# A one-column exponential ahead of ScalarE's third q transfer in an attention and feed-forward kernel

## The chip, the cores and the metric

The kernel runs on one core of a Trainium2 chip. The metric is the device time of one execution in microseconds; lower is better. The time before is the median of three runs, 856.87 us (856.82 to 857.83).

## The reference

Eight batches of eight heads, 576 positions, 64 columns per head. The softmax of q runs over a head's columns, that of k over the positions; attention is linear, and its output goes through a feed-forward layer with a squared ReLU.

```python
q_s = exp(q - max(q, axis=-1)); q_s = q_s / (sum(q_s, axis=-1) + 1e-9)
k_s = exp(k - max(k, axis=2));  k_s = k_s / (sum(k_s, axis=2) + 1e-9)
kv = einsum('bhsd,bhse->bhde', k_s, v)
x = einsum('bhsd,bhde->bhse', q_s, kv)      # as 4608 tokens x 512
h = maximum(x @ w_in, 0.0)                  # w_in 512 x 2048
return (h * h) @ w_out                      # w_out 2048 x 512
```

q, k and v are float32. The weights arrive as float64 and are turned into float32 on the chip.

## The kernel before

Heads are worked on in pairs p = 0 to 3 of each batch b. A batch has 512 positions in main tiles (q_b_p, k_b_p, v_b_p: 128 partitions x 512) and 64 left over in tail tiles for all heads (qt_b, kt_b, v_tail). Every number of the feed-forward matmuls is carried as a rounded part and a rest (names ending in h and l: xh, xl, gh, gl), three matmuls for one product. A token tile has 512 tokens; for each block f of 128 columns of w_in, twelve matmuls make h, ScalarE and VectorE square it, and twelve make its share of acc. The last token tiles are computed from sums and differences of weight blocks (lines 1264 and 1776).

Weights come in 16 units u. Each is two halves of 512 KB (raw_u), which ScalarE scales, VectorE shifts and joins, GpSimd adds (w<-w,raw), ScalarE rounds and GpSimd splits (w<-w,w). Units 0 to 11 lie in the pool const, 12 to 15 in the pool late, which takes the place of the pool boot once the first batch's tiles are done with. SBUF pools are opened in the order const, att, cvt, ffn, tiny, boot (later late); tiny holds small statistics.

The first batch starts the kernel. For it, k's maximum over positions is taken from transposed keys:
- TensorE transposes k_0_p into PSUM (kT) and the tail kt_0 into ktT.
- `first_tail_max`: VectorE reduces ktT to ktm, and ScalarE copies ktT back over kt (two lines below); both read the same PSUM bank, and VectorE's reduction comes behind the copy.
- `first_max`: VectorE reduces kT to kc and joins ktm into it (kc<-kc,ktm).
- `first_exp`: ScalarE computes exp(kT + kc), with its sums.
- `q_max`, `q_exp`: VectorE takes the maximum over q (mx), GpSimd subtracts it (q<-q,mx), ScalarE takes the exponential.

```python
V.tensor_reduce(out=ktm, in_=ps[:, 0:2 * P].rearrange("p (n t) -> p n t", t=TL), op=ALU.max, axis=AX.X, n=256)
S.copy(out=kt, in_=ps[:, 0:2 * P], n=256)
```

The engines are V (VectorE, DVE), S (ScalarE, ACT), G (GpSimd, POOL), T (TensorE, PE) and Y (SyncE, SP). Nearly all transfers are issued by SP; the first batch's q and qt by ScalarE's queue, in the order q_0_0, qt_0 (two halves), q_0_1, q_0_2, q_0_3. Eight transfer semaphores (DMAHW0 to DMAHW7) go round over all issues, so an issue waits until the transfer that had its semaphore before has landed.

The instructions are not issued as they are written. Every call on an engine is recorded (line 100 is the recorder, which is why most rows of the profile bear that line), and a planner orders them by reckoned times: an instruction counts as a fixed part plus a part per column, for ScalarE

```python
V, S, G = Engine(plan, nc.vector, 0.14, 0.00108), Engine(plan, nc.scalar, 0.18, 0.00087), Engine(plan, nc.gpsimd, 0.1, 0.0021)
```

`plan.together()` records several calls as one step, and a list of seeds shifts the ranks of steps by their place in the record. Transfers on one queue keep the order in which they were recorded. Where TensorE would have nothing to do early on, a fixed number of dummy transposes (`idle<-ident`, line 1454) is put in, from the planner's times.

The function table of ScalarE is loaded by an instruction of its own, ACT_TABLE_LOAD, which the compiler puts ahead of the first instruction on ScalarE that is not a transfer.

Of the kernel before, what the change touches and what calls it, by code (L numbers as in the profile page):

```python
# [10 lines left out]
F32 = mybir.dt.float32  # L11
# [4 lines left out]
AF = mybir.ActivationFunctionType  # L16
# [320 lines left out]
def attention_ffn(  # L337
# [29 lines left out]
    P = 128  # L367
# [3 lines left out]
    NP = H // 2  # L371
# [40 lines left out]
    def pool(name, bufs, to=ctx, **more):  # L412
        return Pool(to.enter_context(tc.tile_pool(name=name, bufs=bufs, **more)), bufs)

    const, att, cvt = pool("const", 1), pool("att", 1), pool("cvt", 2)
    ffn, tiny = pool("ffn", 2), pool("tiny", 1)
# [13 lines left out]
    plan = Planner()  # L430

    V, S, G = Engine(plan, nc.vector, 0.14, 0.00108), Engine(plan, nc.scalar, 0.18, 0.00087), Engine(plan, nc.gpsimd, 0.1, 0.0021)
# [7 lines left out]
    ones = const.pool.tile([P, P], F32, tag="ones", name="ones")  # L440
# [100 lines left out]
    def pair_tile(b, p, shape, tag, dtype=F32):  # L541

        two = tag in ("ek", "v")
        pool = boot if b == 0 and p < NP - 1 - two else att
        return pool.tile(shape, dtype, tag=tag, name=f"{tag}_{b}_{p}", bufs=2 if two else None)
# [7 lines left out]
    def load_kq(b, p, which, queue=Y):  # L553
        turned = which == "k" and b == 0
        t = pair_tile(b, p, [P, C, 2, D] if turned else [P, 2, C, D], which)
        src = (k if which == "k" else q)[b, 2 * p:2 * p + 2, 0:M, :]
        to = "p c h d" if turned else "p h c d"
        queue.dma_start(out=t, in_=src.rearrange(f"h (p c) d -> {to}", c=C), kb=256)
        made[which, b, p] = t
# [20 lines left out]
    def load_v(b, p):  # L580
        t = pair_tile(b, p, [P, VW], "v")
        if b == 0:
            t = t[:, 0:2 * C * D].rearrange("p (h c d) -> p h c d", h=2, c=C)
            Y.dma_start(
                out=t, in_=v[b, 2 * p:2 * p + 2, 0:M, :].rearrange("h (p c) d -> p h c d", c=C),
                kb=256,
            )
            made["v", b, p] = t
            return
        t = t[:, 0:C * W].rearrange("p (c w) -> p c w", c=C)  # L590
        (G if b < TB else V).memset(t[:, :, D:D + 1].only("ones"), 1.0, n=4)
        for j in range(2):
            Y.dma_start(
                out=t[:, :, j * (D + 1):j * (D + 1) + D].only(j),
                in_=v[b, 2 * p + j, 0:M, :].rearrange("(p c) d -> p c d", c=C),
                kb=128,
            )
        made["v", b, p] = t
# [697 lines left out]
    load_tail_kq(0, "k")  # L1296
    load_tail_kq(0, "q", S)
    load_kq(0, 1, "k")
    for p in range(1, NP):
        load_kq(0, p, "q", S)  # L1300
    load_v(0, 0)
    load_tail_v(0)
    load_words(0)
# [703 lines left out]
```

## Time and profile before

| what | value |
|---|---|
| median of three runs | 856.87 us |
| the profiled execution: time | 858.72 us |
| the profiled execution: span | 856.92 us |
| mean granted clock of TensorE | 0.998 |
| TensorE busy | 843.8 us, 98% of the span |
| VectorE, ScalarE, GpSimd busy | 631.1, 424.2, 126.4 us |
| moved by DMA | 111.78 MB, mean 130 GB/s |

The profile is one execution. A row of its timeline gives the start and the length in microseconds from the span's start, the engine, the line, the operation, out<-in and how many were merged (x3); brackets hold how long the engine sat idle ahead of it and what ended that. An engine's name with q (ACTq, SPq) is its queue issuing a transfer. Buffer numbers are left out, so k stands for all tiles of k. The chain is followed back from the last instruction to what released it, step by step. A DMA row gives the size of a transfer and the microseconds from issue to landing.

### The profile page before, as it was taken

To read this page: it belongs to the slowest core of one execution; us is meant where nothing else is said; L and a number is where in the kernel's file an instruction comes from. 1 tells how busy PE (TensorE), PEld (TensorE's weight loads), DVE (VectorE), ACT (ScalarE), POOL (GpSimd) and SP (SyncE) were. 2 spreads that over 40 slices of the span, in tenths; PEclk is the share of its full clock that TensorE was granted. 3 is DMA by queue.
4 is the path that set the end of the run, shared out by engine and by line. 5 is a ranking of instruction groups with operands and counts; after the bars stand their busy time and mean duration, and the time that the engine had idled before them with its cause. 6 is when DMAs were issued, how large, how long until landed. Compare 5 with 4: busy or idle time off the path is not lost.

```text
span 856.9 us, 12691 instructions
## 1 busy us (share of the span) xinstructions
PE 843.8 (98%) x4356; PEld 697.1 (81%) x4356; DVE 631.1 (74%) x1241; ACT 424.2 (50%) x794; POOL 126.4 (15%) x154
## 2 busy tenths in 40 slices
PE   7899999999999999999999999999999999999997
PEld 6688888888888888888888888888888888888886
DVE  5898887776776677777686777776767756777985
ACT  4888864343534344433534344334533536666442
POOL 5789981000000000000000000000000000000000
PEclk9999999999999999999999999999999999999999
DMA  9991122323531443233432341132351039979565
GB/s 288 384 352 41 36 60 85 88 78 77 143 98 31 138 106 107 73 86 89 132 90 69 108 144 40 40 90 58 89 134 40 5 114 323 301 275 376 150 182 96
DMA packets 192752, 111.78 MB, mean 130 GB/s; under 512 B 130736, under 2 KB 175792, under 8 KB 192688
## 3 DMA queue, kind: packets, MB, share of 16 engines
q1 hardware_dynamic: 186768, 109.27, 43.2%
q10 hardware_dynamic: 5920, 1.71, 0.8%
q8 instruction: 34, 0.56, 0.3%
q14 instruction: 30, 0.25, 0.1%
HBM read 73.79 MB, written 36.57 MB: 129 GB/s over the span
## 4 chain that ended last, share of the span: by engine, by line
PE 92%; DVE 2%; POOL 1%; DMA 1%; ACT 1%; issue 0%; SPq 0%; DVEq 0%; ACTq 0%; POOLq 0%
PE h L100 35%; PE acc L100 35%; PE h L1264 9%; PE out L1776 8%; PE x L100 3%; PE kv L100 2%; DMA out_dram<-o 0%; DVE bst L100 0%; POOL w L100 0%; SPq L100 0%; POOL qn L100 0%; PE qT L100 0%; DMA bst<-bst 0%; DVE kvl L100 0%; DVE q L100 0%
## 5 line engine op out<-in xcount | busy, mean ns | idle before, releaser
L100 PE MATMUL h<-xh,w 128*128 128x512 f32 x896 | 296.6, 393 | 0.0
L100 PE MATMUL acc<-w,gh 128*128 128x512 f32 x888 | 274.6, 390 | 0.0
L100 PEld LDWEIGHTS h<-xh,w 128*128 128x128 f32 x896 | 168.7, 188 | 35.4
L100 PEld LDWEIGHTS acc<-w,gh 128*128 128x128 f32 x888 | 165.2, 188 | 33.2
L100 PE MATMUL h<-xl,w 128*128 128x512 f32 x448 | 175.0, 391 | 0.0
L100 PE MATMUL acc<-w,gl 128*128 128x512 f32 x444 | 172.8, 389 | 0.0
L100 DVE TENSOR_TENSOR gl<-h,gh 128x512 fp32r<-128x512 f32 x111 | 76.3, 688 | 59.3 <-ACT gh L100 52.5
L100 ACT ACTIVATE gh<-r 128x512 fp32r<-128x512 f32 x111 | 70.0, 631 | 77.8 <-PE acc L100 76.5
L100 PEld LDWEIGHTS h<-xl,w 128*128 128x128 f32 x448 | 84.4, 188 | 16.6 <-DVE xl L100 0.2
L100 PEld LDWEIGHTS acc<-w,gl 128*128 128x128 f32 x444 | 83.3, 188 | 17.6
L100 DVE SCALAR_TENSOR_TENSOR h<-h,r 128x512 f32<-128x512 f32 x112 | 77.2, 690 | 24.9 <-ACT r L100 24.0
L100 ACT ACTIVATE r<-h 128x512 f32<-128x512 f32 x112 | 66.5, 593 | 58.1 <-PE h L100 57.9
L100 POOL PARTITION_ALL_REDUCE kmx<-km x24 | 16.9, 705 | 507.4 <-DVE km L100 507.4
L1776 PE MATMUL out<-w,w 128*128 128x512 f32 x324 | 75.7, 389 | 0.0
L1776 PEld LDWEIGHTS out<-w,w 128*128 128x128 f32 x324 | 60.8, 188 | 12.6
L100 ACT ACTIVATE q<-q 128x576 f32<-128x576 f32 (+1 forms) x32 | 21.5, 672 | 69.7 <-DVE q L100 66.2
L100 DVE TENSOR_REDUCE bst<-q 128x18 f32<-128x576 f32 x48 | 35.9, 748 | 14.2 <-ACT q L100 13.5
L100 POOL TENSOR_TENSOR w<-w,raw 128x512 int32<-128x512 int32 x32 | 42.2, 1324 | 4.7 <-ACT raw L100 2.0
L100 POOL TENSOR_TENSOR w<-w,w 128x512 fp32r<-128x512 f32 x32 | 41.4, 1307 | 5.0 <-ACT w L100 2.9
L100 DVE TENSOR_TENSOR q<-q,bst 128x576 f32<-128x576 f32 x48 | 36.4, 758 | 1.7
L100 ACT ACTIVATE raw<-raw 128x1024 f32<-128x1024 f32 (+1 forms) x32 | 36.2, 1152 | 0.1
L1264 PE MATMUL h<-w,w 128*128 128x512 f32 x144 | 34.7, 389 | 0.0
(205 smaller groups left out, 1054.4 us busy)
## 6 DMA issues: line engine op xcount, KB each, us to landing
k<-in_k_dram SPq DMA_DIRECT2D x32, 256.0 KB, 2.9
raw<-in_moe_w_in_dram SPq DMA_DIRECT2D x16, 512.0 KB, 7.8
raw<-in_moe_w_out_dram SPq DMA_DIRECT2D x16, 512.0 KB, 8.8
w<-wo_sums SPq DMA_DIRECT2D x32, 256.0 KB, 3.8
w_sums<-w SPq DMA_DIRECT2D x30, 256.0 KB, 3.1
g_b<-c SPq DMA_DIRECT2D x30, 256.0 KB, 4.1
v<-in_v_dram SPq DMA_DIRECT2D x56, 128.0 KB, 3.0
out_dram<-o SPq DMA_DIRECT2D x28, 256.0 KB, 2.2
```

The source lines that it names most:

```text
L100: getattr(self.eng, op)(*map(real, args), **{k: real(a) for k, a in kwargs.items()})
L1264: nc.tensor.matmul(out=out.real(), lhsT=a[:, k * P:(k + 1) * P].real(), rhs=m[k].real(), start=(begin and k == 0 and i == 0), stop=(k == 1 ...
L1776: nc.tensor.matmul(out=banks[name][m].real(), lhsT=a[:, m * P:(m + 1) * P].real(), rhs=b[:, i, :].real(), start=fresh and j == i == k == 0 ...
```

## The change

A tile `warm` of one column is added to the pool tiny, and ScalarE writes the exponential of a column of ones into it. The call is recorded as one step with the issue of q_0_2. Its column count of -207 makes it cost 0.18 - 207 x 0.00087 = 0.00 in the planner's reckoning, and the number of steps stays the same.

```diff
     load_kq(0, 1, "k")
-    for p in range(1, NP):
-        load_kq(0, p, "q", S)
+    load_kq(0, 1, "q", S)
+    with plan.together():
+        warm = tiny.pool.tile([P, 1], F32, tag="warm", name="warm")
+        S.activation(out=warm, in_=ones[:, 0:1], func=AF.Exp, n=-207)
+        load_kq(0, 2, "q", S)
+    load_kq(0, 3, "q", S)
     load_v(0, 0)
```

On ScalarE, the start of the program before (names have the tile's number behind them, DMAHW, PE, DVE and Pool in the brackets are the semaphores it waits for):

```order
L100 DMA q_0_0_145<-in_q_dram 128x2x256
L100 DMA qt_0_149<-in_q_dram 64x4x64 x2
L100 DMA q_0_1_155<-in_q_dram 128x2x256
L100 DMA q_0_2_157<-in_q_dram 128x2x256 [waits DMAHW0_49]
L100 DMA q_0_3_161<-in_q_dram 128x2x256 [waits DMAHW2_49]
L100 ACT_TABLE_LOAD [waits DMAHW5_49,DMAHW3_49]
L100 COPY kt_0_147<-ktT_187 128x256 [waits PE_49]
L100 ACTIVATE q_0_0_145<-q_0_0_145 128x512 [waits Pool_49]
```

And ScalarE at the same place now:

```order
L100 DMA q_0_1_156<-in_q_dram 128x2x256
L100 ACT_TABLE_LOAD
L100 ACTIVATE warm_142<-ones_91 128x1 [waits DVE_49]
L100 DMA q_0_2_159<-in_q_dram 128x2x256 [waits DMAHW0_49]
L100 DMA q_0_3_163<-in_q_dram 128x2x256 [waits DMAHW2_49]
L100 COPY kt_0_148<-ktT_189 128x256 [waits DMAHW5_49,DMAHW3_49,PE_49]
L100 ACTIVATE q_0_0_146<-q_0_0_146 128x512 [waits Pool_49]
```

The table load, of which there is one in either program, has moved ahead of two transfers and no longer waits for the kt transfers; the copy waits for them and for TensorE.

On SP, whose rows are the same before and now but for the tiles' numbers, the transfer of v_0_1 waits for DMAHW0, which q_0_2 had before it, and that of v_0_2 for DMAHW2, which q_0_3 had:

```order
L100 DMA raw_0_182<-in_moe_w_in_dram 128x4x128 [waits DMAHW6_49]
L100 DMA k_0_2_197<-in_k_dram 128x8x64 [waits DMAHW7_49]
L100 DMA v_0_1_210<-in_v_dram 128x2x256 [waits DMAHW0_49]
L100 DMA k_0_3_214<-in_k_dram 128x8x64 [waits DMAHW1_49]
L100 DMA v_0_2_222<-in_v_dram 128x2x256 [waits DMAHW2_49]
L100 DMA v_0_3_226<-in_v_dram 128x2x256 [waits DMAHW3_49]
L100 DMA raw_1_250<-in_moe_w_in_dram 128x4x128 [waits DMAHW4_49]
L100 DMA raw_1_250<-in_moe_w_out_dram 128x512 [waits DMAHW5_49]
```

Nothing on SP has moved. On TensorE, VectorE and GpSimd too the instructions stand in the same order, with the same waits and the same number of dummy transposes. The new tile takes 32 bytes of each partition at the start of the pool tiny, behind a pad; the tiles of tiny, boot and late start 32 bytes later, those of boot and late at odd multiples of 32 bytes where they started at multiples of 64. All other tiles lie where they lay.

## The prediction

> **What bounds the kernel now.** I read the page's busy shares and chain first, then the chain in order of time, then the instructions of the first 40 us engine by engine.
>
> ```profile
> PE 843.8 (98%) x4356; PEld 697.1 (81%) x4356; DVE 631.1 (74%) x1241; ACT 424.2 (50%) x794; POOL 126.4 (15%) x154
> PE 92%; DVE 2%; POOL 1%; DMA 1%; ACT 1%; issue 0%; SPq 0%; DVEq 0%; ACTq 0%; POOLq 0%
> ```
>
> TensorE is busy for 98% of the span and makes up 92% of the chain that ended last, so a change that leaves its instructions alone can only move the point from which it runs without a gap. The chain in order of time shows where that is.
>
> ```profile
> 37.69 0.85 PE x L100 x2
> ...
> 55.41 2.72 PE h L100 x12
> ...
> 60.96 2.77 PE h L100 x12
> ```
>
> From 37.69 on the chain is TensorE; before that it hops between engines. The question is therefore what the first 38 us wait for, and whether the table load is part of it. The timeline of the start:
>
> ```profile
> 4.93 1.11 PE L100 MATMUL kT<-ident,k 128*128 128x128 f32 x4 [0.97 <-DMA k<-in_k_dram]
> ...
> 6.08 0.69 DVE L100 TENSOR_REDUCE kc<-kT 128x1 f32<-128x512 f32 x1 [1.71 <-PE kT L100]
> ...
> 6.95 1.28 ACT L100 ACT_TABLE_LOAD   x1 [6.95 <-DMA kt<-in_k_dram]
> ...
> 6.99 0.66 PE L100 MATMUL ktT<-ident,kt 128*128 128x128 f32 x2 [0.31 <-DMA kt<-in_k_dram]
> ...
> 8.25 0.37 ACT L100 COPY kt<-ktT 128x256 f32<-128x256 f32 x1
> ...
> 8.65 0.43 DVE L100 TENSOR_REDUCE ktm<-ktT 128x4 f32<-128x256 f32 x1 [1.55 <-ACT kt L100]
> ...
> 9.75 1.04 POOL L100 TENSOR_TENSOR q<-q,mx 128x512 f32<-128x512 f32 x1 [4.24 <-DVE ktm L100]
> 9.78 1.03 DVE L100 SCALAR_TENSOR_TENSOR kc<-kc,ktm 128x1 f32<-128x1 f32 x1
> ...
> 10.84 0.69 ACT L100 ACTIVATE k<-kT,kc 128x512 f32<-128x512 f32 x1 [1.70 <-DVE kc L100]
> ```
>
> The load waits for the kt transfers and starts with the transposes ktT that wait for the same. The transposes end at 6.99 + 0.66 = 7.65; the load holds ScalarE until 6.95 + 1.28 = 8.23, and the copy of ktT starts at 8.25. VectorE's ktm stands behind that copy (idle 1.55, released by ACT kt), and behind ktm everything down to the first exponential of k at 10.84, on which ScalarE waits 1.70. So the part of the load that the transposes do not cover is on the path.
>
> **What the change removes there.** Without the load in front of it the copy waits for ktT alone. In the kT rows a reader of PSUM starts 6.08 - (4.93 + 1.11) = 0.04 after the last transpose, so the copy would start at 7.65 + 0.04 = 7.69: 8.25 - 7.69 = 0.56 earlier. ktm follows the copy's start by 0.40 now, and comes at 8.09. The rest of the piece keeps its distances: the reduction behind ktm needs q_0_1, which was there long before (issued at 2.58 and landed 4.6 later, at 7.2; rows below). kc's 1.03 for a 128x1 operand is the time for which GpSimd's subtraction beside it runs (it starts 0.03 sooner and ends at 10.79); both hang on the same reduction, so this meeting is kept, shifted. The exponential of k starts near 10.28.
>
> Does the 0.56 live until 37.69? Later waits of the same chain, in order:
>
> ```profile
> 17.25 0.20 PEld L100 LDWEIGHTS qTt<-ident,qt 128*128 128x128 f32 x2 [1.78 <-DVE qt L100]
> ...
> 19.49 1.15 ACT L100 ACTIVATE kvh<-kv,ks 64x64 fp32r<-64x64 f32 x4 [2.16 <-PE kv L100]
> ...
> 20.16 1.10 DVE L100 SCALAR_TENSOR_TENSOR kvl<-kv,ks,kvh 64x64 fp32r<-64x64 f32 x4 [1.15 <-ACT kvh L100]
> ```
>
> Each waits for an engine, none for a transfer, so each moves with its releaser. What could stop the shift is a transfer that lands at a fixed time. The first two weights are the nearest:
>
> ```profile
> 7.93 0.51 SPq L100 DMA_DIRECT2D raw<-in_moe_w_in_dram  x1
> ...
> 15.18 2.15 ACT L100 ACTIVATE raw<-raw 128x1024 f32<-128x1024 f32 x2
> 15.19 0.51 SPq L100 DMA_DIRECT2D raw<-in_moe_w_out_dram  x1
> ...
> 22.29 1.17 ACT L100 ACTIVATE raw<-raw 128x1024 f32<-128x1024 f32 x1
> ```
>
> and the times to landing of the two transfers issued there, from the list of transfers:
>
> ```profile
> raw<-in_moe_w_in_dram SPq DMA_DIRECT2D x1, 512.0 KB, 6.1
> ...
> raw<-in_moe_w_out_dram SPq DMA_DIRECT2D x1, 512.0 KB, 5.6
> ```
>
> raw_0 has landed at 7.93 + 6.1 = 14.0 and would be used at 15.18 - 0.56 = 14.62; raw_1 at 15.19 + 5.6 = 20.8, used at 21.73. Margins of 0.6 and 0.9, so the shift passes.
>
> **What it adds.** One exponential over 128x1, and the load, both now between q_0_1 and q_0_2 on ScalarE's queue.
>
> ```profile
> 2.58 0.62 ACTq L100 DMA_DIRECT2D q<-in_q_dram  x1
> 3.69 0.37 ACTq L100 DMA_DIRECT2D q<-in_q_dram  x1
> 5.18 0.37 ACTq L100 DMA_DIRECT2D q<-in_q_dram  x1
> ...
> 12.71 0.34 ACT L100 ACTIVATE kt<-kt,kc 128x64 f32<-128x64 f32 x1
> ```
>
> Those are the issues of q_0_1, q_0_2, q_0_3 and the nearest row to the new exponential. The times to landing of q_0_0, q_0_1, q_0_2, q_0_3, from the list of transfers:
>
> ```profile
> q<-in_q_dram ACTq DMA_DIRECT2D x1, 256.0 KB, 2.9
> ...
> q<-in_q_dram ACTq DMA_DIRECT2D x1, 256.0 KB, 4.6
> ...
> q<-in_q_dram ACTq DMA_DIRECT2D x1, 256.0 KB, 5.1
> ...
> q<-in_q_dram ACTq DMA_DIRECT2D x1, 256.0 KB, 5.5
> ```
>
> The load can start at 2.58 + 0.62 = 3.20 and ends at 4.48. The exponential's input, ones, has long been set; the nearest row takes 0.34 for 64 columns; for one I take 0.27, so ScalarE is free at 4.75. Whether an issue waits for work in hand on its engine no row shows: q_0_2 goes out between 3.69 (it does not) and 4.75 (it does); I reckon with 4.75, 1.06 late. q_0_3 waits for the first qt transfer and goes out at 5.18 or just behind.
>
> What the late issue costs: q_0_2 took 5.1 to land and q_0_0, alone in its queue, 2.9, so q_0_2 stood 2.2 behind others. A delay of 1.06 fits into that, and the landing stays near 3.69 + 5.1 = 8.79; at worst it is 9.85. Two wait for it: VectorE's maximum over q_0_2, now at 11.86 and then at 11.30, and, through the shared semaphore DMAHW0, the issue of v_0_1 on SP, with the keys and weights behind it.
>
> ```profile
> 9.15 2.43 SPq L100 DMA_DIRECT2D v<-in_v_dram  x1
> ...
> 11.62 0.63 SPq L100 DMA_DIRECT2D k<-in_k_dram  x1
> ...
> 11.86 0.69 DVE L100 TENSOR_REDUCE mx<-q 128x8 f32<-128x512 f32 x1
> ```
>
> The maximum has 1.4 to spare even at 9.85. v_0_1's issue starts at 9.15, 0.36 behind the landing, and takes 2.43 where k's takes 0.63: something else holds it until 11.58. A start at up to 9.85 need not end later. I put 0 for the queue, between 0 and +0.7 on SP, of which raw_1's margin of 0.9 takes all.
>
> The Trainium skill (ScalarE: Activation LUTs, What ACT_TABLE_LOAD costs) puts about 1.38 us of drain onto a load of 1.28, 2.66 in all. The row here has the copy 0.02 behind the load's end, so no drain shows at this first load. By that figure of the Trainium skill, as an estimate, the sum would keep its 0.56 and q_0_2 would go out at 6.1 instead of 4.75, landing near 9 by the same queueing, which changes nothing in the time.
>
> **The sum.** The profiled execution took 858.72, with a span of 856.92, 1.8 around it. Its span becomes 856.92 - 0.56 = 856.4, the same execution 858.2. Carried over to the median of the runs before, 856.87, that is 856.3; its own range is 856.1 (another 0.2 from transfers that give way to each other) to 856.6 (half of it lost to the dummy transposes, whose count stays and which TensorE must finish ahead of the real ones behind them).
>
> **Rivals.** First, nothing arrives: a margin above is smaller than a single profile shows, or TensorE's own conditions absorb 0.56. For it speaks that 0.56 is small against the stages between; against it, that no wait from 8.65 to 37.69 in the rows names a transfer. 856.9.
>
> Second, slower by TensorE's clock. The windows at the start of the gapless part:
>
> ```profile
> 34.28:37.69 3.41, 2.17 (x27) 1.00 1.09 335
> 37.69:41.10 3.41, 3.41 (x10) 0.50 1.07 391
> ...
> 40.34 0.63 PE L100 MATMUL h<-xh,w 128*128 128x512 f32 x1
> 40.77 0.55 PE L100 MATMUL h<-xl,w 128*128 128x512 f32 x1
> ```
>
> (Length, TensorE busy, granted clock, DMA.) After a window with 2.17 of 3.41 busy, a window of the same length is granted half the clock: matmuls start 0.43 apart, against 2.72 / 12 = 0.227 later. That costs at most 3.41 x (1 - 0.227 / 0.43) = 1.6. The Trainium skill (TensorE: Matmul & The Clock Gate, Part 1) calls this window free-running, 3413 ns long; the length agrees, the free running no single trace can show. If the shift moves the thin stretch fully into one window in runs that were spared before, the time is 856.3 + 1.6 = 857.9. It decides where a window ends between some 37 and 38 us. That the unprofiled runs spread over 1.0 us, 856.82 to 857.83, speaks for such a lottery.
>
> Third, the same mechanism the other way: the earlier start brings real matmuls into the window that ends at 37.69, the half clock is not imposed, and 856.3 - 1.6 = 854.7. Against it: the two lower runs before (856.82 and 856.87) may already have been without it, as they are 1.9 below the profiled execution.
>
> Fourth, the SP queue undoes the gain. If q_0_2 lost its place and landed no sooner than q_0_3 does, at 5.18 + 5.5 = 10.7, and v_0_1's issue moved whole, SP would stand 10.7 - 9.15 = 1.55 later, 0.65 beyond raw_1's margin of 0.9, and ScalarE would wait for raw_1: 856.3 + 0.65 = 857.0. It needs both, and the 2.2 of queueing speaks against the first.
>
> Fifth, placement. The new tile takes 32 bytes, so the tiles of boot and late start at odd multiples of 32 instead of multiples of 64. Late holds a quarter of the weights.
>
> ```profile
> L100 PE MATMUL kv<-v,ek x64: 222/222/271, 17.6 to 35.7; 128*64 128x64 f32 x64
> ...
> L100 PE MATMUL kv<-v,ek x448: 220/222/272, 68.5 to 664.6; 128*64 128x65 f32 x150
> ```
>
> The first group reads v at multiples of 256 bytes; in the second v's rows are 129 floats, so most start off any such multiple. Medians are 222 and 222 ns, so an operand's start costs TensorE nothing here. If it did, by the spread of 2.77 against 2.72 per 12 matmuls, 4 ns on a quarter of the 4356 matmuls would be 4.4 at most: 860.7.
>
> **Chances.** Forecast 0.56; nothing arrives 0.15; clock worse 0.12; clock better 0.08; SP queue 0.04; placement 0.05. A measurement of this kernel can tell about 0.2%, 1.7 us, from no change: below 855.16 is faster, above 858.58 slower. Faster holds the better clock, 0.08; slower the placement and the edge of the worse clock, 0.06; the same 0.86. The range 855.0 to 858.0 leaves out the better clock and the placement, 0.13, and takes in the others.
>
> **What would show it.** In the changed profile: the load near 3.2 with no idle time in front of the copy but ktT's; the copy at 7.7, ktm at 8.1, k's exponential near 10.3; q_0_2 issued at 3.7 to 4.8; v_0_1 issued not later than 9.9, and k behind it at 11.6; raw_0 and raw_1 used 0.5 earlier; the first gapless x matmul near 37.1. The forecast is wrong if ktm moves and 37.69 does not, if a wait before 37 names a transfer, if kc no longer meets GpSimd's subtraction (0.87 more gained), or if the half clock lies elsewhere or is missing.

## The result and the profile after

| | before | after |
|---|---|---|
| median | 856.89 us (856.77 to 858.13, 6 runs) | 862.63 us (862.35 to 864.1, 6 runs) |
| the profiled execution: time, span | 858.72, 856.9 | 862.83, 861.0 |

The changed kernel is slower: the ratio (time after over time before) is 1.0066, with a 95% interval of 1.0053 to 1.0079. That is 5.7 us more, where the prediction had 0.6 less.

The start of the changed kernel, from its timeline (start, length, engine; idle time and releaser in brackets):

```profile
2.60 0.62 ACTq L100 DMA_DIRECT2D q<-in_q_dram  x1
3.25 1.28 ACT L100 ACT_TABLE_LOAD   x1 [3.25 <-issue]
3.61 0.38 ACTq L100 DMA_DIRECT2D q<-in_q_dram  x1
4.54 0.20 ACT L100 ACTIVATE warm<-ones 128x1 f32<-128x1 f32 x1
...
6.61 0.66 PE L100 MATMUL ktT<-ident,kt 128*128 128x128 f32 x2
7.31 0.37 ACT L100 COPY kt<-ktT 128x256 f32<-128x256 f32 x1 [2.56 <-PE ktT L100]
7.71 0.42 DVE L100 TENSOR_REDUCE ktm<-ktT 128x4 f32<-128x256 f32 x1 [0.63 <-ACT kt L100]
...
8.84 1.02 DVE L100 SCALAR_TENSOR_TENSOR kc<-kc,ktm 128x1 f32<-128x1 f32 x1
...
9.28 1.86 SPq L100 DMA_DIRECT2D v<-in_v_dram  x1
9.90 0.69 ACT L100 ACTIVATE k<-kT,kc 128x512 f32<-128x512 f32 x1 [1.69 <-DVE kc L100]
```

This stage does what was forecast. The load is out of the way, and the copy now waits for ktT alone: it starts 0.70 behind the start of the transposes, where it was 8.25 - 6.99 = 1.26, so the 0.56 is there to the hundredth. (Everything stands another 0.38 earlier than forecast, because kt landed sooner in this execution; the other profiles, of kernels without the exponential, have ktT anywhere from 6.62 to 7.38.)

The chain of the changed kernel, in order of time (start, length, engine, tile, line, instructions merged):

```profile
36.97 0.53 PE x L100 x2
...
38.58 6.17 PE h L100 x27
...
618.08 2.72 PE h L100 x12
...
679.61 2.79 PE h L100 x12
682.40 2.80 PE acc L100 x12
685.20 2.79 PE h L100 x12
687.99 2.80 PE acc L100 x12
```

and of the kernel before, at the same place of the program:

```profile
683.69 2.72 PE h L100 x12
686.41 2.72 PE acc L100 x12
689.13 2.72 PE h L100 x12
```

The gapless part starts earlier than before (36.97 against 37.69), and then TensorE itself is slower. Twelve matmuls over 512 columns take 2.72 us before, at 683 as at 55; after, some blocks still take 2.72 (618.08) and others 2.79 or 2.80. No wait stands between them. The blocks of 2.79 and 2.80 are those whose weights lie in the pool late. The same is seen in the busy time of TensorE and of the largest groups (busy us, mean ns of one), before:

```profile
PE 843.8 (98%) x4356; PEld 697.1 (81%) x4356; DVE 631.1 (74%) x1241; ACT 424.2 (50%) x794; POOL 126.4 (15%) x154
...
L100 PE MATMUL acc<-w,gh 128*128 128x512 f32 x888 | 274.6, 390 | 0.0
...
L1776 PE MATMUL out<-w,w 128*128 128x512 f32 x324 | 75.7, 389 | 0.0
```

and after, with as many matmuls:

```profile
PE 849.3 (99%) x4356; PEld 697.4 (81%) x4356; DVE 631.1 (73%) x1241; ACT 425.0 (49%) x795; POOL 126.4 (15%) x154
...
L100 PE MATMUL acc<-w,gh 128*128 128x512 f32 x888 | 276.1, 392 | 0.0
...
L1780 PE MATMUL out<-w,w 128*128 128x512 f32 x324 | 77.1, 393 | 0.0
```

A group's mean mixes matmuls of both paces. So I sorted the matmuls over 512 columns by where their operands lie (the programs give each operand's tile and address), and took the median of the times from one start to the next. w12 to w15 are late's four weight tiles; the moving operand is the one whose 512 columns stream through, the stationary one is loaded by LDWEIGHTS.

| operand in late | matmuls | before, ns | after, ns |
|---|---|---|---|
| none | 2433 | 227 | 227 |
| moving | 506 | 227 | 234 |
| stationary | 382 | 227 | 232 |
| both | 38 | 227 | 229 |

506 x 7 + 382 x 5 + 38 x 2 = 5.5 us, close to the 5.7 of the medians. It is a sum of medians: added up one by one against the profile before, without intervals over 300 ns, the matmuls with an operand in late give 5.1 us and the 2433 others 1.1, more than half of that behind 680 us. Why some of those others are slower too stays open. What the exponential itself did is not in this table at all.

### The profile page after: what moved, and what is told of

Same layout as the page of the kernel before. It is cut to its first block, busy times and chain, and to the rows that moved or that the text cites. A ratio compares the mean times of both kernels' runs of the same rounds, so it can differ in the third digit from the quotient of the medians.

```text
span 861.0 us, 12692 instructions
## 1 busy us (share of the span) xinstructions
PE 849.3 (99%) x4356; PEld 697.4 (81%) x4356; DVE 631.1 (73%) x1241; ACT 425.0 (49%) x795; POOL 126.4 (15%) x154
## 4 chain that ended last, share of the span: by engine, by line
PE 91%; DVE 2%; DMA 1%; POOL 1%; SPq 1%; ACT 1%; issue 0%; DVEq 0%; ACTq 0%; POOLq 0%
PE acc L100 34%; PE h L100 34%; PE out L1780 9%; PE h L1264 9%; PE x L100 3%; PE kv L100 2%; SPq L100 1%; DVE bst L100 1%; DMA bst<-bst 0%; DVE q L100 0%; DMA k<-in_k_dram 0%; POOL w L100 0%; DVE km L100 0%; POOL qn L100 0%; PE qT L100 0%
```

## The experiments

Theories: the loss is due to the 32 bytes by which the tiles of boot and late moved (the prediction's fifth rival), or to the earlier load and the clock. Four kernels took the change apart. They ran on one chip, where the kernel before had a median of 857.78 us.

**The exponential without the shift.** The changed kernel, with tiny's pad cut by the 32 bytes that warm takes:

```diff
-    tiny.pool.tile([P, 68], F32, tag="pad2", name="pad2")
+    tiny.pool.tile([P, 60], F32, tag="pad2", name="pad2")
```

> The changed kernel, with the pad ahead of the tile warm made 32 bytes smaller, so that every other tile lies where it lay before the change. Placement theory (the loss comes from the tiles of late standing 32 bytes off): the loss is gone and the early table load is left alone, 855.9 to 856.4 against 856.9 before; 12 matmuls on late's weights take 2.72 again. Order theory (the loss comes from the moved table load and the later q transfers): about 862.6, as the changed kernel. No third value fits either.

857.91 us, ratio 1.0000 [0.9992, 1.0009]. The loss is gone, and no gain shows. Its chain has late's blocks at the old pace, and starts without a gap at 37.43:

```profile
37.43 0.85 PE x L100 x2
...
683.54 2.72 PE h L100 x12
686.26 2.72 PE acc L100 x12
```

**The shift without the exponential.** The kernel before, with tiny's pad 32 bytes longer:

```diff
-    tiny.pool.tile([P, 68], F32, tag="pad2", name="pad2")
+    tiny.pool.tile([P, 76], F32, tag="pad2", name="pad2")
```

> The kernel before, with the same pad 32 bytes larger: tiny, boot and late start 32 bytes later as in the changed kernel, and no exponential is added. Placement theory: the loss alone without the gain of the early load, 862.9 to 863.7; matmuls with a late operand start 232 to 234 ns apart where others keep 227. Order theory: 856.9.

863.93 us, ratio 1.0070 [1.0057, 1.0083]: the whole loss, without a changed instruction.

**Late alone, and boot alone.** The first has the kernel before with the pad at late's head 32 bytes longer, the second has tiny and boot 32 bytes later and late where it was:

```diff
-        late.pool.tile([P, 16], F32, tag="pad3", name="pad3")
+        late.pool.tile([P, 24], F32, tag="pad3", name="pad3")
```
```diff
-    tiny.pool.tile([P, 68], F32, tag="pad2", name="pad2")
+    tiny.pool.tile([P, 76], F32, tag="pad2", name="pad2")
...
-        late.pool.tile([P, 16], F32, tag="pad3", name="pad3")
+        late.pool.tile([P, 8], F32, tag="pad3", name="pad3")
```

> The kernel before, with late alone moved by 32 bytes. If the price lies in the matmuls that read late's weights, the same as with tiny and boot moved too, 862.9 to 863.7. If part of it lies in the tiles of boot (transfers, transposes and exponentials of the first batch) or of tiny, less than that by this part, at the least 856.9.

> The kernel before, with tiny and boot moved by 32 bytes and late left in its place. By the late operand: 856.9, no change. By boot or tiny: what the run with late alone lacks, up to 863. If the transfers into boot's tiles got slower, the kt transfers land later than 6.9 us and ktT starts later than 6.99.

Late alone: 863.25 us, ratio 1.0068 [1.0055, 1.0080]. Boot alone: 857.62 us, ratio 1.0001 [0.9992, 1.0010], with ktT at 6.79, no later than before. The position of four weight tiles is the whole loss. The chain with late alone moved:

```profile
679.69 2.79 PE h L100 x12
682.48 2.80 PE acc L100 x12
```

**What about the position costs?** "Odd multiples of 32" is only one reading of it. The other operands of the matmuls (const, cvt, ffn) start at multiples of 256 bytes, and so did late. Theory A: an operand pays for its own start. Theory B: the two operands of a matmul pay when they start at different places within some unit. Three kernels, on a chip where before had 857.60 us: late 64 bytes later (pad3 of 32 columns), every tile 32 bytes later, and all but tiny, boot and late 32 bytes later.

```diff
-    const.pool.tile([P, 32], F32, tag="pad", name="pad")
+    const.pool.tile([P, 40], F32, tag="pad", name="pad")
```

(in the kernel with every tile moved; the complement of late has this and tiny's pad at 60).

> The kernel before with late's tiles 64 bytes later (even multiples of 32 again, but no longer multiples of 128). Theory A, an operand costs more when it starts off a multiple of 64 bytes: no loss, 857.8 within 0.9. Theory C, what counts is a larger boundary (128 bytes or more): a loss as with 32 bytes, 863.3.

> The kernel before with every tile on the chip 32 bytes later, so that all operands of all matmuls start at odd multiples of 32. Theory A (each operand pays by its own start): nearly all of the some 4000 matmuls over 512 columns pay 5 to 7 ns instead of a quarter of them, so 20 to 28 us more, 878 to 886; if a matmul with both operands off pays less than with one, as the few such matmuls of the changed kernel's trace (1 to 6 ns) may say, 862 to 882. Theory B (what counts is that the two operands of a matmul stand at different places within 64 bytes): none differ, so no loss, 857.8 within 0.9.

> The kernel before with every tile but those of boot, late and the small ones 32 bytes later: the complement of the shift of late alone. Theory A: each matmul has at least one operand off, some 20 to 28 us more, 878 to 886, or what both operands off give. Theory B: only the quarter of the matmuls that read late's weights has unlike operands, as with late alone, 863.3.

The chain of the three, late at 64 first:

```profile
681.42 2.76 PE acc L100 x12
684.18 2.80 PE h L100 x12
```

every tile at 32:

```profile
38.68 0.53 PE x L100 x2
...
683.44 2.72 PE h L100 x12
686.16 2.72 PE acc L100 x12
```

all but late at 32:

```profile
684.73 2.80 PE acc L100 x12
687.53 2.80 PE h L100 x12
```

Late at 64 costs nearly as much, 862.36 us, ratio 1.0053 [1.0034, 1.0071]; a multiple of 64 is not enough. With every tile at an odd multiple of 32 no matmul is held up: 2.72 per twelve, 227 ns in every row of the table above. Theory A, by which nearly all of them would have been slower, is out. With all but late moved, late's blocks are at 2.80 again, though late itself lies where it lay, and all other matmuls, both of whose operands are at odd multiples of 32, keep their 227 ns. So theory B holds for the matmuls: what counts is how the operands lie to each other.

One row of the first table seems to speak against it: with both operands in late they start alike, and yet the median after is 229. The weights of the next matmul count as well. In the changed kernel, 22 matmuls have operands that start alike, but a moving operand that starts unlike the next one's weights; their median is 235, and was 227 before. The 48 with their own weights unlike and the next one's alike have 233, and where both are alike it is 227 (2386 matmuls). With late at 64 the same 22 stay at 226 and the 48 have 231, so this second part depends on the offset.

The times of these two miss theory B's numbers, however: 860.06 us, ratio 1.0033 [1.0016, 1.0050], where it said 857.8, and 865.88 (four runs, one of them 871.28, which widens the interval), ratio 1.0110 [1.0067, 1.0153], where it said 863.3; some 2.5 us more in either. That is not on the matmuls' pace. About 1 of it stands at the end: from the start of the last matmul to the end of the span it is 6.08 and 6.07, in the nine other profiles 4.98 to 5.26. A late store of the result takes longer in the chain, with every tile moved:

```profile
847.04 3.48 DMA out_dram<-o
```

with all but late moved:

```profile
852.60 3.67 DMA out_dram<-o
```

where before it takes

```profile
848.40 2.48 DMA out_dram<-o
```

and 2.36 to 2.69 in the six other chains that hold it. In the list of transfers, the kernel with every tile moved has

```profile
raw<-in_moe_w_in_dram SPq DMA_DIRECT2D x16, 512.0 KB, 9.1
raw<-in_moe_w_out_dram SPq DMA_DIRECT2D x16, 512.0 KB, 9.8
wo_sums<-sums_o SPq DMA_DIRECT2D x8, 512.0 KB, 4.5
```

The first and the third are slower than in any of the nine other profiles, which have 7.8 to 8.5 and 4.0 to 4.1; the second is not (8.8 to 10.0). The remaining 1.5 is open: in the two profiles the waits lie on different transfers (one of w_sums, 5.57, and one of q, 6.70). That transfers pay for the position by themselves fits this; no run tried it alone.

The late gapless start of the kernel with every tile moved, 38.68 - 7.04 = 31.64 behind the start of ktT where seven profiles have 30.66 to 30.70, is not the position. In this execution the clock was halved at 19.08 (a window: length; busy time and count of TensorE, its weight loads, VectorE, ScalarE and GpSimd; granted clock; DMA share; GB/s):

```profile
19.08:22.50 3.42, 3.42 (x24) 3.24 (x19) 1.68 (x5) 2.38 (x8) 2.45 (x4) 0.50 1.08 376
```

With all but late moved there is no such window, and the gapless part starts 38.06 - 7.38 = 30.68 behind ktT.

**How large is the unit?** Late 128 bytes later (pad3 of 48 columns; before 858.38 us there), and 256 bytes later (80 columns; before 857.49):

> The kernel before with late's tiles 128 bytes later, so that they differ from the other operands by 128 bytes within 256 instead of not at all. The shift of 32 cost 5.5 us (6.3 ns per matmul that streams late's weights), that of 64 cost 4.8 (4 ns). Theory D, what counts is the difference of the two operands within 128 bytes: no loss, 857.6 within 0.9, and all matmuls 227 ns apart. Rival, the difference counts within a larger unit (256 bytes or more): a loss again, of the 2 to 5 us that the step from 32 to 64 lets expect.

> The kernel before with late's tiles 256 bytes later. In the kernel before they lie 256 bytes off the other operands within 512 (and equal within 256). Theory, the difference counts within 256 bytes: no loss, all matmuls 227 ns apart, the time of before within 0.9 us. Rival, any move of late against the other operands costs, or the unit is larger than 256: a loss of 4 to 6 us again.

Late at 128:

```profile
682.85 2.77 PE acc L100 x12
685.63 2.79 PE h L100 x12
```

late at 256:

```profile
679.26 2.72 PE acc L100 x12
681.98 2.72 PE h L100 x12
```

862.91 us, ratio 1.0054 [1.0037, 1.0071], and 857.42, ratio 1.0003 [0.9993, 1.0012]. Theory D of the first of these two expectations, a unit of 128 bytes, is out; a move by 256 costs nothing. Offsets of 32, 64 and 128 bytes between the operands cost, 0 and 256 do not. By operand and offset, median ns from start to start:

| late moved by | moving in late | stationary in late | none in late |
|---|---|---|---|
| 0, 256 | 227 | 227 | 227 |
| 32 | 234 | 232 | 227 |
| 64 | 231 | 233 | 227 |
| 128 | 232 | 232 | 227 |

## Why the prediction was wrong

**The step that failed** is the fifth rival, which had the right place, the right sign and a chance of 0.05. It named the moved tiles and their quarter of the weights, and dismissed them with "an operand's start costs TensorE nothing here", from kv matmuls that took 222 ns whether v lay at a multiple of 256 bytes or not. Those rows could not show it, for three reasons. Their 222 ns are lengths of single matmuls, while what the shift changed is the distance from one start to the next: a feed-forward matmul is 389 ns long before, and starts 227 behind the one before it. They are matmuls over 64 or 65 columns, not 512. And a row of 129 floats is 516 bytes, 4 more than a multiple of 256, so over the four rows v starts 0, 4, 8 or 12 bytes off the start of ek, never 32. The fair test was a row of the same kind, and the profile of before held none, since all operands of its 512-column matmuls lie alike within 256 bytes. That is an unknown cost, to be bounded from both sides and kept in the range; the row that bounded it was of another kind.

**The size** was bounded at 4 ns on a quarter of 4356 matmuls, 4.4 us. Measured: 7 ns on 506 matmuls, 5 on 382 and 2 on 38, 5.5 us. The spread of 2.77 against 2.72 in the profile of before, from which the 4 ns came, has nothing to do with it: such blocks of 2.77 stand in the profiles with and without the shift.

**The place of the unit** was wrong too: the prediction spoke of odd multiples of 32 against multiples of 64. An offset of 64 or 128 costs as well, and odd multiples of 32 cost the matmuls nothing if all operands share them.

The rest, point by point:

- *The load and the copy.* Right: 3.25 to 4.53 (forecast 3.20 to 4.48), copy 0.04 behind ktT's end, ktm 0.40 behind the copy, kc still 1.02 beside GpSimd's subtraction, the first exponential of k at 9.90, which is 10.28 less the 0.38 by which kt landed sooner.
- *The exponential.* 0.20, reckoned 0.27; it starts 0.01 behind the load.
- *The issue of q_0_2.* Wrong, without effect. It went out at 3.61, in the middle of the load. Nothing held it; even the lower bound of 3.69 was too late. v_0_1 was issued at 9.28, and nothing on SP came late by it: the 0 for the queue stands.
- *Does the 0.56 reach TensorE?* Only in part, and not reliably. The start of the gapless part behind the start of ktT is 30.66 to 30.70 in seven profiles without the exponential and at full clock until then. With it, it is 36.97 - 6.61 = 30.36 in the changed kernel, 0.33 gained, and 37.43 - 6.64 = 30.79 without the shift, 0.1 lost. In the latter a transfer is in the way:

```profile
22.59 1.15 ACT L100 ACTIVATE raw<-raw 128x1024 f32<-128x1024 f32 x1 [1.00 <-DMA raw<-in_moe_w_out_dram]
```

  This is the wait on raw_1 for which the prediction saw a margin of 0.9. It took the margin from one execution's landing of 5.6; here the transfer, issued at 15.26, let ScalarE go only 7.3 later. So the first rival (a margin smaller than one profile shows) describes that execution, at 0.15. In the changed kernel the first scaled kv (kvh) stands 18.77 - 6.61 = 12.16 behind ktT, before 19.49 - 6.99 = 12.50, so its missing 0.2 was lost ahead of that; on what, I leave open. In the times neither sign can be told from zero: the interval of the version without the shift is about 0.8 us wide on either side.
- *The clock.* The lottery that the second and third rivals rest on is real. The changed kernel has no half-clock window at its gapless start; the version without the shift has one, 0.36 before the place it had before (columns as in the window above):

```profile
37.33:40.74 3.41, 3.31 (x10) 2.92 (x11) 3.09 (x7) 2.89 (x6) 2.74 (x4) 0.50 1.06 349
```

  and the shift without the exponential has it in another stage, as has the kernel with every tile moved:

```profile
19.35:22.76 3.41, 3.41 (x19) 3.41 (x18) 1.86 (x6) 2.91 (x8) 2.07 (x4) 0.50 0.97 253
```

  These two windows are 18.0 us apart, no whole number of 3.41. The Trainium skill (TensorE: Matmul & The Clock Gate, Part 1) calls the window free-running; these profiles agree. At the gapless start it is worth 1.5 us in a single execution: the first 71 matmuls from there on take 16.86 from the first start to the last before, 15.34 in the changed kernel. Neither rival decided this result.
- *The range and the chances.* 855.0 to 858.0 left out the fifth rival by its chance; it ended 4.6 above the range.

## What to carry to other kernels

An edit that only adds a small tile also moves every tile behind it. Ahead of weighing its instructions, list which operands of the bounding engine's instructions change their start, and keep those of one matmul alike within 256 bytes: a pad of 256 bytes cost no time here, and the right place is worth ten times what the edit could have brought. Where the profile holds no row of the same kind of instruction with the new placement, the cost is unknown, and a row of another kind with another limit bounds nothing.

## What the runs showed of the hardware

- Matmuls over 512 columns start 227 ns apart when their two operands start alike within 256 bytes, and 231 to 234 ns apart when they differ by 32, 64 or 128 bytes, whichever of the two is the odd one. The Trainium skill (SBUF — State Buffer, Operand start alignment) asks only for a multiple of the element's size, and says itself that this is about legality, not speed; every kernel here keeps to it, and the two paces differ by up to 3%. Both the matmul's own weights and the next one's count (233 and 235 ns at 32 bytes); why they do, no run shows.
- The kernel whose tiles all lie at odd multiples of 32 lost some 2.5 us outside the matmuls' pace, 1 of it behind the last matmul (6.08 against 4.98 to 5.26). Some transfers landed later (9.1 us against 7.8 to 8.5 for the first halves of the weights).
- ScalarE's queue issued a transfer at 3.61, while its function table was loading (3.25 to 4.53).
- A window of 3.41 us at half the clock came at 37.69, 37.33, 19.35 or 19.08 in four of eleven profiles, and at none of these places in the others.
